# Moving the cache loads of a decode-attention kernel from GpSimd's DMA queue to SyncE's, and the last load of wo behind the last values

## The chip, the cores and the metric

The kernel runs on one core of a Trainium2 chip (eight cores, of which seven stay idle here). The metric is the device time of one execution in microseconds, as a median over runs. The profile is one further execution, recorded by the hardware profiler; its span runs from the first to the last instruction, so it is a little shorter than the execution itself.

## The reference

One decode step: one token of width D = 640 attends over a cache of 32768 positions in 32 heads of width 192, and then passes through a small dense block. Everything is bfloat16.

```python
x: (1, 1, 640)   k_cache, v_cache: (1, 32, 32768, 192)   wq: (640, 32*192)   wo: (32*192, 640)
w1: (640, 1536)  w2: (1536, 640)

q = (layernorm(x) @ wq).reshape(1, 1, 32, 192).transpose(0, 2, 1, 3)
scores = einsum("bhqd,bhkd->bhqk", q, k_cache) * 192 ** -0.5
o = einsum("bhqk,bhkd->bhqd", softmax(scores), v_cache)
h = x + o.transpose(0, 2, 1, 3).reshape(1, 1, 32 * 192) @ wo
h2 = h + relu(layernorm(h) @ w1) @ w2
```

The two caches are 805 MB of the 825 MB that the kernel reads. Each byte is used once, for one query.

## The kernel before

The work is staged head by head: `LAST` = 31 is the last of heads 0 to 31. Head h reads its keys in two loads, k(h,0) and k(h,1), of 6,144 KB each, into the buffers `kt[0]` and `kt[1]`, and its values in three: v(h,0) and v(h,1), of 3,072 KB each, both into the buffer `vb`, and v(h,2), of 6,144 KB, into `va`. There is one buffer of each, so a load waits until the work on what the buffer held is done. A head is computed in eight chunks c = 0 to 7, four on each key buffer. Of each chunk one part of the scores is formed on VectorE (`scores_dve`, L714 and L717: a product with the query, then a sum) and the other part on TensorE (`transposes` at L390, copied out of PSUM by ScalarE at L617, then `scores_pe`, recorded at L371). ScalarE forms the exponentials (L623 and L632), and TensorE multiplies them with the values (`values`, recorded at L371 with output `o_ps`); the end of that is the event PV(h,c). Chunks 0 and 1 use v(h,0), chunks 2 and 3 use v(h,1), chunks 4 to 7 use v(h,2). In head 0 the order of the values on TensorE is 0, 1, 4, 5, 2, 3, 6, 7 (`SUMS_0`).

All order is written out by hand. Each engine runs its own program, and `wait` names the event that it waits for. What matters here is the two programs without arithmetic:

- `relay_program`, on SyncE: first it issues seven loads (`first_loads`, L235): the five parts of wq, then k(0,0) and v(0,0). After that it waits for each load in turn and tells TensorE (L353) and VectorE (L332) that it has landed.
- `dma_program`, on GpSimd: after building an identity matrix it issues all other loads (L250), with `single_packet=True`, each behind the waits for its buffer.

The waits of the loads that the prediction follows are these. k(0,1) and v(0,2) wait until the queries are done (`att0`), since they overwrite wq. v(h,1) waits for PV(h,1). k(1,0) waits for PV(0,4) and for VectorE's chunk 3 of head 0 (`scs`). v(1,0) waits for PV(0,3). k(1,1) waits for PV(0,5) and VectorE's chunk 7.

wo comes in 16 loads of 480 KB into one buffer `wo_s`, one for every two heads, issued at the even heads. The last head has smaller pieces: keys k(31,0) to k(31,5), values v(31,0) and v(31,1), two halves of v(31,2) and four small pieces behind; then w1 and four parts of w2. Its program on TensorE (`pe_end`) ends with the projection through wo (`project`), the second norm, w1, and w2.

Of the kernel before, what the change touches and what calls it, by code (L numbers as in the profile page):

```python
# [7 lines left out]
A = mybir.AluOpType  # L8
# [72 lines left out]
def kernel(  # L81
# [12 lines left out]
    nc = tc.nc  # L94
    P = nc.NUM_PARTITIONS

    Bsz, Sq, D = A_x.shape
    _, H, Sk, Dh = A_k_cache.shape
# [6 lines left out]
    DT = D // P  # L105
    FT = Dff // P
    JK = 128
    JL = 64
    J = 32
    JPS = (20, 16)  # L110
    HE = Dh // 2
    NK = Sk // (P * JK)
# [3 lines left out]
    LAST = H - 1  # L116
# [26 lines left out]
    k_hd = A_k_cache.rearrange("b h s d -> (b h) s d")  # L143
    v_hd = A_v_cache.rearrange("b h s d -> (b h) s d")
    wq_view = A_wq.rearrange("(p c) n -> p (c n)", p=P)
    wo_view = A_wo.rearrange("(g p b) n -> g p b n", p=P, b=3)
# [4 lines left out]
    def sbuf(name, shape, dtype, align=32):  # L151
        return ctx.enter_context(nc.sbuf_tensor(name, shape, dtype, align_bytes=align))
# [5 lines left out]
    kt = [sbuf(f"kt{i}", [P, JK * Dh], bf16, 512) for i in range(NK)]  # L158
    va = sbuf("va", [P, JK * Dh], bf16, 512)
    vb = sbuf("vb", [P, JL * Dh], bf16, 512)  # L160
    wo_s = sbuf("wo_s", [P, 3, D], bf16, 512)
# [10 lines left out]
    wide = sbuf("wide", [P, HE + P + 2 * (P - HE)], bf16)  # L172
# [29 lines left out]
    wq_c = [kt[1][:, c * H * Dh:(c + 1) * H * Dh] for c in range(DT - 1)] + [va[:, 0:H * Dh]]  # L202
# [14 lines left out]
    def v_tile(h, ld):  # L217
        return v_at[ld] if h == LAST else (vb, vb, va)[ld][:]


    names = ["pool_pe", "act_pe", "dve_pe", "act_dve", "dve_act", "dve", "dve_row", "pe_dve", "pool_row", "pool_dve", "pool_act", "pe_act", "pe", "dve_sp", "act_row"]
    names += [f"dk{i}" for i in range(NK)] + ["dva", "dvb", "dk_first", "dv_first"] + ["dwo", "dx", "dout"] + [f"dwq{i}" for i in range(5)]
    names += [f"dke{i}" for i in range(4)] + ["dvh0", "dvh1"] + [f"dve{i}" for i in range(4)] + ["dw1"] + [f"dw2_{i}" for i in range(4)]
    sems = {n: nc.alloc_semaphore(n) for n in names}

# [1 line left out]
             "dve": ("pool_dve", "act_dve", "pe_dve", "dve")}  # L227


    def rows(src, h, k0, jl):  # L230
        return src[h, k0:k0 + P * jl, :].rearrange("(p j) d -> p (j d)", p=P)

    def first_loads(g):
        def load(dst, src, sem, *label):
            g.do(lambda: nc.sync.dma_start(out=dst, in_=src), sem, label, by=16)  # L235

        for c in range(DT):
            load(wq_c[c], wq_view[:, c * H * Dh:(c + 1) * H * Dh], f"dwq{c}", "wq", c)
        load(kt[0][:], rows(k_hd, 0, 0, JK), "dk_first", "k", 0, 0)
        load(vb[:], rows(v_hd, 0, 0, JK)[:, 0:JL * Dh], "dv_first", "v", 0, 0)  # L240

    def dma_program(g):
        e = nc.gpsimd
        g.do(lambda: e.memset(wide[:], 0.0), "pool_act", ("ident0",))
        g.wait("ident0")
        g.do(lambda: e.affine_select(out=wide[:], in_=wide[:], compare_op=A.not_equal, fill=1.0, base=HE,
                                     pattern=[[-1, HE + P + 2 * (P - HE)]], channel_multiplier=1), "pool_row", ("ident",))

        def load(dst, src, sem, *label):
            g.do(lambda: e.dma_start(out=dst, in_=src, single_packet=True), sem, label, by=16)  # L250

        def keys(h, ld):
            if h > 0:
                if ld == 0:
                    g.wait("PV", h - 1, 4 if h == 1 else 2)
                else:
                    g.wait("PV", h - 1, 5)
                g.wait("scs", h - 1, 4 * ld + 3)
            elif ld == 1:
                g.wait("att0")  # L260
            load(kt[ld][:], rows(k_hd, h, P * JK * ld, JK), f"dk{ld}", "k", h, ld)

        def vals(h, ld):

            if ld == 1:
                g.wait("PV", h, 1)
            elif h > 0:
                g.wait("PV", h - 1, 3 if ld == 0 else NC - 1)
            src = rows(v_hd, h, P * JK * (ld // 2), JK)
            if ld < 2:  # L270
                src = src[:, ld * JL * Dh:(ld + 1) * JL * Dh]
            load((vb, vb, va)[ld][:], src, "dva" if ld == 2 else "dvb", "v", h, ld)

        for h in range(LAST):
            if h > 0:
                keys(h, 0)
                vals(h, 0)
            keys(h, 1)
            for ld in ((2, 1) if h == 0 else (1, 2)):
                vals(h, ld)  # L280
            if h % 2 == 0:
                if h > 0:
                    g.wait("prj", h)
                load(wo_s[:], wo_view[h // 2], "dwo", "wo", h // 2)

        def end_keys(i, k0, jl, sem):
            load(k_at[i], rows(k_hd, LAST, k0, jl), sem, "k", LAST, i)

        def end_values(ld, c0, c1, sem, *label):
            load(v_at[ld][:, c0:c1], rows(v_hd, LAST, P * JL * ld, JL)[:, c0:c1], sem, *label)  # L290


        g.wait("PV", LAST - 1, 2)
        g.wait("scs", LAST - 1, 3)
        end_keys(0, 0, JL, "dk0")
        g.wait("PV", LAST - 1, 3)
        end_values(0, 0, JL * Dh, "dvb", "v", LAST, 0)
        end_keys(1, P * JL, JL, "dke0")
        g.wait("PV", LAST - 1, 5)
        g.wait("scs", LAST - 1, NC - 1)  # L300
        end_keys(2, 2 * P * JL, JL, "dk1")
        k0 = P * JL * (NL - 1)
        at = []
        for i, jl in enumerate(ENDJ):
            at.append((k0, jl))
            end_keys(NL - 1 + i, k0, jl, f"dke{1 + i}")
            k0 += P * jl
        g.wait("PV", LAST - 1, NC - 1)
        end_values(1, 0, JL * Dh, "dva", "v", LAST, 1)

        for i in range(2):
            end_values(2, i * J * Dh, (i + 1) * J * Dh, f"dvh{i}", "vh", i)
        i = 0
        for ld, (k0, jl) in enumerate(at):
            for c, (l, off, jc, *_) in enumerate(ends):
                if l == NL - 1 + ld:
                    g.wait("PV", LAST, 1)
                    load(v_tile(LAST, l)[:, off * Dh:(off + jc) * Dh],
                         rows(v_hd, LAST, k0, jl)[:, off * Dh:(off + jc) * Dh], f"dve{i}", "vc", LAST, c)
                    i += 1  # L320
        g.wait("PV", LAST, 3)
        load(w1_s, B_w1.rearrange("(c p) n -> p c n", p=P), "dw1", "w1")
        for i, (c0, c1) in enumerate(zip(W2_CUTS[:-1], W2_CUTS[1:])):
            load(w2_s[:, c0:c1], B_w2.rearrange("(c p) n -> p c n", p=P)[:, c0:c1], f"dw2_{i}", "w2", i)


    def relay_program(g):
        first_loads(g)

        def key(h, ld):  # L330
            relay(g, "k", h, ld)
            g.do(lambda: nc.sync.sem_inc(sems["pool_dve"], 1))  # L332
            book_relay(g, "k", h, ld, sem="pool_dve")

        for h in range(LAST):
            key(h, 0)
            relay(g, "v", h, 0)
            key(h, 1)
            for ld in ((2, 1) if h == 0 else (1, 2)):
                relay(g, "v", h, ld)  # L340
            relay(g, "W", h)
        key(LAST, 0)
        relay(g, "v", LAST, 0)
        key(LAST, 1)
        key(LAST, 2)
        relay(g, "v", LAST, 1)

    def relay(g, *label):
        if label[0] != "W":
            g.wait(*label)  # L350
        elif label[1] % 2 == 0:
            g.wait("wo", label[1] // 2)
        g.do(lambda: nc.sync.sem_inc(sems["pool_pe"], 1))  # L353
        book_relay(g, *label)

    def book_relay(g, *label, sem="pool_pe"):
        if g.planning:
            n = g.book["count"].get(sem, 0) + 1
            g.book["count"][sem] = n
            g.book["at"][("at" if sem == "pool_pe" else "atd",) + label] = (sem, n)  # L360
# [445 lines left out]

    book = {"count": {}, "at": {}}
    plan = Program(book, sems)
    for f in (relay_program, dma_program):
        f(plan)  # L810
    parts = {"pe": (pe_start, pe_head, pe_end), "act": (act_start, act_head, act_end), "dve": (dve_start, dve_head, dve_end)}
    logs, links = {}, {}
# [56 lines left out]
    with nc.Block(name="decode_blk", no_gpsimd_drain=True) as block:  # L869
        @block.sync  # L870
        def _(eng):
            relay_program(Program(book, sems, nc.sync))

        @block.gpsimd
        def _(eng):
            dma_program(Program(book, sems, nc.gpsimd))

        @block.scalar
        def _(eng):
            looped("act", nc.scalar)  # L880

        @block.vector
        def _(eng):
            looped("dve", nc.vector)

        @block.tensor
        def _(eng):
            looped("pe", nc.tensor)
# [34 lines left out]
```

## Time and profile before

| | |
|---|---|
| median of 4 runs | 1920.84 us (1919.93 to 1921.7) |
| the profiled execution | 1923.71 us, of which the span is 1921.8 us |
| busy share of the span | PE 81%, DVE 81%, PEld 57%, ACT 49%, POOL 5% |
| mean granted TensorE clock | 0.874 |
| read from HBM | 824.97 MB, 429 GB/s over the span |
| queue q0 (software_dynamic: GpSimd's) | 25984 packets, 807.68 MB, 97.4% of 16 DMA engines' span |
| queue q1 (hardware_dynamic: SyncE's) | 1008 packets, 17.30 MB, 2.1% |
| issue of one 6,144 KB load | 0.48 us on SyncE, 0.53 us on GpSimd |

PE is TensorE's matmuls, PEld its weight loads, DVE is VectorE, ACT ScalarE, POOL GpSimd, SP SyncE; a q behind a name (SPq) is the engine's sequencer, which handles waits and signals. Times in the rows are microseconds from the start of the span. "Idle before" is the time in which an engine stood still ahead of an instruction, with what released it. The chain is followed back from the last instruction: each step was released by the one before it.

### The profile page before, as it was taken

The page shows a single profiled execution, that of the slowest core. Times are in us where ns is not written, and L with a number is a line of the kernel's source. Part 1 is how long each engine was busy: PE and PEld are TensorE (multiplying, and loading weights), DVE is VectorE, ACT ScalarE, POOL GpSimd, SP SyncE. Part 2 cuts the span into 40 slices and gives each one's busy share as a digit, 9 for nine tenths or more (in the row PEclk, how much of TensorE's full clock was granted, in tenths as well). Part 3 has the DMA queues.
Part 4 walks back from the last instruction along what each step waited for, and adds up shares of the span by engine and source line. Part 5 has one row for each costly group of instructions (what it writes and reads, how often), then busy time and mean ns, then how long its engine had stood idle before and what let it go on. Part 6 is the DMA issues. An engine that isn't in the chain of part 4 may idle for free.

```text
span 1921.8 us, 36109 instructions
## 1 busy us (share of the span) xinstructions
PE 1560.9 (81%) x15899; PEld 1092.5 (57%) x15899; DVE 1561.3 (81%) x731; ACT 939.3 (49%) x2000; POOL 101.6 (5%) x194
## 2 busy tenths in 40 slices
PE   7687887888878888878878787788778787878888
PEld 7455555655555565555555555555555555555555
DVE  2888788987879878789787888878798787887896
ACT  1454454553545544545545445545355454454454
POOL 0000000000000000000000000000000000000011
PEclk9889988788988889888899888998888998888998
DMA  9999999999999999999999999999999999999998
GB/s 409 388 434 430 430 436 429 437 435 428 437 430 438 428 439 429 437 430 437 434 433 433 435 434 433 435 429 438 429 436 434 434 434 433 435 432 434 430 433 350
DMA packets 27026, 825.29 MB, mean 429 GB/s; under 512 B 3131, under 2 KB 3132, under 8 KB 5500
## 3 DMA queue, kind: packets, MB, share of 16 engines
q0 software_dynamic: 25984, 807.68, 97.4%
q1 hardware_dynamic: 1008, 17.30, 2.1%
q8 instruction: 15, 0.25, 0.0%
q14 instruction: 7, 0.06, 0.0%
q10 hardware_dynamic: 12, 0.00, 0.0%
HBM read 824.97 MB, written 0.00 MB: 429 GB/s over the span
## 4 chain that ended last, share of the span: by engine, by line
DVE 39%; DMA 36%; PE 16%; ACT 5%; issue 2%; another core or an unknown queue 1%; DVEq 0%; SPq 0%; POOL 0%
DMA kt<-in_A_k_cache_dram 36%; DVE sc L717 19%; DVE pr L714 18%; PE tp L390 8%; PE o_ps L371 7%; ACT kT L617 5%; PE sp L371 1%; DVE o_pair L729 1%; ACT pA L632 1%; DVE oT L739 0%; DVE rec L722 0%; DVE rec L723 0%; DVE odd L735 0%; DVE o_pair L741 0%
## 5 line engine op out<-in xcount | busy, mean ns | idle before, releaser
L714 DVE TENSOR_TENSOR pr<-kt,qb 128x2304 f32<-128x2304 bf16 (+2 forms) x257 | 756.7, 2944 | 318.9 <-SPq L332 290.8
L617 ACT COPY kT<-tp 128x1024 bf16<-128x1024 bf16 (+1 forms) x898 | 814.3, 1017 | 275.8 <-PE tp L390 275.8
L390 PE MATMUL tp<-ident_f,kt 128*128 128x128 f32 x3456 | 595.2, 333 | 240.8 <-SPq L353 165.6
L717 DVE TENSOR_REDUCE sc<-pr 128x12 f32<-128x2304 f32 (+2 forms) x257 | 756.1, 2942 | 8.9
L390 PEld LDWEIGHTS tp<-ident_f,kt 128*128 128x128 f32 x3456 | 488.4, 172 | 291.7 <-SPq L353 171.0
L371 PE MATMUL o_ps<-va,pB 128*2 128x384 bf16 x1152 | 219.2, 338 | 49.1 <-SPq L353 49.1
L371 PE MATMUL o_ps<-vb,pB 128*2 128x384 bf16 x1152 | 219.1, 337 | 34.7 <-ACT pA L632 20.4
L371 PEld LDWEIGHTS sp<-qm,kT 128*128 128x128 bf16 x6912 | 197.6, 98 | 83.7 <-issue 43.1
L371 PE MATMUL sp<-qm,kT 128*128 128x2 bf16 x6912 | 214.8, 164 | 25.4 <-ACT pB L623 24.0
L632 ACT ACTIVATE pA<-sc 128x12 bf16<-128x12 f32 (+2 forms) x257 | 58.1, 226 | 341.9 <-DVEq L65 341.9
L623 ACT ACTIVATE pB<-sp 128x20 bf16<-128x20 f32 (+2 forms) x258 | 52.4, 203 | 315.8 <-PE sp L371 315.8
L371 PEld LDWEIGHTS o_ps<-va,pB 128*2 128x2 bf16 x1152 | 93.7, 86 | 143.8 <-SPq L353 56.3
L371 PE MATMUL o_ps<-va,pA 128*2 128x384 bf16 x896 | 170.8, 332 | 0.0
L371 PEld LDWEIGHTS o_ps<-vb,pB 128*2 128x2 bf16 x1152 | 91.4, 86 | 139.0 <-ACT pA L632 27.4
L371 PE MATMUL o_ps<-vb,pA 128*2 128x384 bf16 x896 | 167.7, 327 | 0.0
L371 PEld LDWEIGHTS o_ps<-va,pA 128*2 128x2 bf16 x896 | 76.9, 86 | 74.7 <-issue 7.3
L371 PEld LDWEIGHTS o_ps<-vb,pA 128*2 128x2 bf16 x896 | 75.4, 84 | 70.9 <-issue 1.2
L250 POOL DMA_DIRECT2D kt<-in_A_k_cache_dram x67 | 35.6, 531 | 835.9 <-PE o_ps L371 804.6
L250 POOL DMA_DIRECT2D vb<-in_A_v_cache_dram x66 | 34.9, 529 | 811.5 <-PE o_ps L371 811.5
L623 ACT ACTIVATION_READ_ACCUMULATOR pB<-sp 128x1 f32 x258 | 55.1, 214 | 0.0
L632 ACT ACTIVATION_READ_ACCUMULATOR pA<-sc 128x1 f32 x257 | 53.0, 206 | 0.0
L371 PE MATMUL o_ps<-xn_ln,kt 128*96 128x1 bf16 (+1 forms) x316 | 22.3, 208 | 2.6 <-DMA kt<-in_A_wq_dram 2.6
(74 smaller groups left out, 260.0 us busy)
## 6 DMA issues: line engine op xcount, KB each, us to landing
kt<-in_A_k_cache_dram POOLq DMA_DIRECT2D x61, 6144.0 KB, 26.1
va<-in_A_v_cache_dram POOLq DMA_DIRECT2D x31, 6144.0 KB, 26.4
vb<-in_A_v_cache_dram POOLq DMA_DIRECT2D x62, 3072.0 KB, 13.2
kt<-in_A_k_cache_dram POOLq DMA_DIRECT2D x3, 3072.0 KB, 22.8
wo_s<-in_A_wo_dram POOLq DMA_DIRECT2D x16, 480.0 KB, 18.7
kt<-in_A_wq_dram SPq DMA_DIRECT2D x4, 1536.0 KB, 10.9
kt<-in_A_k_cache_dram SPq DMA_DIRECT2D x1, 6144.0 KB, 36.0
vb<-in_A_v_cache_dram SPq DMA_DIRECT2D x1, 3072.0 KB, 57.2
```

The source lines that it names most:

```text
L250: g.do(lambda: e.dma_start(out=dst, in_=src, single_packet=True), sem, label, by=16)
L371: return lambda: pe.matmul(o, lhsT=w, rhs=r, **kw)
L390: calls.append(lambda b=b, o=o: pe.transpose(out=dst[:, b, :], in_=src[:, o:o + 2 * P].bitcast(f32), identity=ident_f[:]))
L617: g.do(lambda: act.copy(out=kT[c % 2][:, b0:b0 + nb, :], in_=src[:, 0:nb, :].bitcast(bf16)), "act_pe", ("cp", h, c, k))
L623: g.do(lambda: act.activation(out=pB[c % NB][:, 0:jp], in_=sp[:, 0:jp], func=F.Exp, scale=SCALE, accum_out=dsums[:, 2 * c + 1:2 * c + 2]), ...
L632: g.do(lambda: act.activation(out=pA[c % NB][:, 0:jd], in_=sc[c % NC][:, 0:jd], func=F.Exp, scale=SCALE, accum_out=dsums[:, 2 * c:2 * c + ...
L714: g.chain(lambda: dve.tensor_tensor(out=pr[:, 0:j1 - j0, :], in0=src[:, (off + j0) * Dh:(off + j1) * Dh].rearrange("p (j d) -> p j d", d=D ...
L717: g.chain(lambda: dve.reduce_sum(out=sc[c % NC][:, j0:j1], in_=pr[:, 0:j1 - j0, :], axis=X), "dve")
L729: g.do(lambda: dve.tensor_scalar_mul(out=o_pair[:, :, 1, :], in0=o_ps[0:2, 0:2 * Dh].rearrange("q (i d) -> q i d", i=2), scalar1=rec[0:2, ...
```

## The change

All loads are issued by SyncE, without the flag, in one queue; the seven first ones stand at the head of the same program (`dma_program`), and their order and the order of all others is what it was. GpSimd takes over the relays (`pool_program`), behind its identity matrix. k(0,0) and v(0,0) lose their own semaphores and share those of the later loads of their buffers. The last load of wo, which was issued at head 30 ahead of k(31,0), is issued behind the last pieces of head 31's values and ahead of w1; the relay that head 30 sent for it no longer waits for it, and the projection at the very end waits for the load itself, as before.

```diff
-    def rows(src, h, k0, jl): ...
-    def first_loads(g):
+    def dma_program(g):
         def load(dst, src, sem, *label):
             g.do(lambda: nc.sync.dma_start(out=dst, in_=src), sem, label, by=16)
 
-        for c in range(DT):
-            load(wq_c[c], wq_view[:, c * H * Dh:(c + 1) * H * Dh], f"dwq{c}", "wq", c)
-        load(kt[0][:], rows(k_hd, 0, 0, JK), "dk_first", "k", 0, 0)
-        load(vb[:], rows(v_hd, 0, 0, JK)[:, 0:JL * Dh], "dv_first", "v", 0, 0)
-
-    def dma_program(g):
-        e = nc.gpsimd
-        (memset and affine_select of the identity)
-        def load(dst, src, sem, *label):
-            g.do(lambda: e.dma_start(out=dst, in_=src, single_packet=True), sem, label, by=16)
+        def rows(src, h, k0, jl): ...
...
+        for c in range(DT):
+            load(wq_c[c], wq_view[:, c * H * Dh:(c + 1) * H * Dh], f"dwq{c}", "wq", c)
         for h in range(LAST):
-            if h > 0:
-                keys(h, 0)
-                vals(h, 0)
+            keys(h, 0)
+            vals(h, 0)
             keys(h, 1)
             for ld in ((2, 1) if h == 0 else (1, 2)):
                 vals(h, ld)
-            if h % 2 == 0:
+            if h % 2 == 0 and h < LAST - 1:
                 if h > 0:
                     g.wait("prj", h)
                 load(wo_s[:], wo_view[h // 2], "dwo", "wo", h // 2)
...
+        g.wait("prj", LAST - 1)
+        load(wo_s[:], wo_view[H // 2 - 1], "dwo", "wo", H // 2 - 1)
         g.wait("PV", LAST, 3)
         load(w1_s, B_w1.rearrange("(c p) n -> p c n", p=P), "dw1", "w1")
...
-    def relay_program(g):
-        first_loads(g)
+    def pool_program(g):
+        (memset and affine_select of the identity)
         def key(h, ld):
             relay(g, "k", h, ld)
-            g.do(lambda: nc.sync.sem_inc(sems["pool_dve"], 1))
+            g.do(lambda: nc.gpsimd.sem_inc(sems["pool_dve"], 1))
...
-        elif label[1] % 2 == 0:
+        elif label[1] % 2 == 0 and label[1] < LAST - 1:
             g.wait("wo", label[1] // 2)
-        g.do(lambda: nc.sync.sem_inc(sems["pool_pe"], 1))
+        g.do(lambda: nc.gpsimd.sem_inc(sems["pool_pe"], 1))
...
         @block.sync
-            relay_program(Program(book, sems, nc.sync))
+            dma_program(Program(book, sems, nc.sync))
         @block.gpsimd
-            dma_program(Program(book, sems, nc.gpsimd))
+            pool_program(Program(book, sems, nc.gpsimd))
```

More of the change, by code (lines that the diff above doesn't have):

```diff
@@ L221 @@
     names = ["pool_pe", "act_pe", "dve_pe", "act_dve", "dve_act", "dve", "dve_row", "pe_dve", "pool_row", "pool_dve", "pool_act", "pe_act", "pe", "dve_sp", "act_row"]
-    names += [f"dk{i}" for i in range(NK)] + ["dva", "dvb", "dk_first", "dv_first"] + ["dwo", "dx", "dout"] + [f"dwq{i}" for i in range(5)]
+    names += [f"dk{i}" for i in range(NK)] + ["dva", "dvb"] + ["dwo", "dx", "dout"] + [f"dwq{i}" for i in range(5)]
     names += [f"dke{i}" for i in range(4)] + ["dvh0", "dvh1"] + [f"dve{i}" for i in range(4)] + ["dw1"] + [f"dw2_{i}" for i in range(4)]
@@ L227, with rows @@
              "dve": ("pool_dve", "act_dve", "pe_dve", "dve")}
-    def rows(src, h, k0, jl):
-        return src[h, k0:k0 + P * jl, :].rearrange("(p j) d -> p (j d)", p=P)
-    def first_loads(g):
+    def dma_program(g):
         def load(dst, src, sem, *label):
             g.do(lambda: nc.sync.dma_start(out=dst, in_=src), sem, label, by=16)
-        for c in range(DT):
-            load(wq_c[c], wq_view[:, c * H * Dh:(c + 1) * H * Dh], f"dwq{c}", "wq", c)
-        load(kt[0][:], rows(k_hd, 0, 0, JK), "dk_first", "k", 0, 0)
-        load(vb[:], rows(v_hd, 0, 0, JK)[:, 0:JL * Dh], "dv_first", "v", 0, 0)
-    def dma_program(g):
-        e = nc.gpsimd
[L244 to L247, printed above, removed]
-        def load(dst, src, sem, *label):
-            g.do(lambda: e.dma_start(out=dst, in_=src, single_packet=True), sem, label, by=16)
+        def rows(src, h, k0, jl):
+            return src[h, k0:k0 + P * jl, :].rearrange("(p j) d -> p (j d)", p=P)
         def keys(h, ld):
@@ L324, in dma_program @@
             load(w2_s[:, c0:c1], B_w2.rearrange("(c p) n -> p c n", p=P)[:, c0:c1], f"dw2_{i}", "w2", i)
-    def relay_program(g):
-        first_loads(g)
+    def pool_program(g):
+        e = nc.gpsimd
+        g.do(lambda: e.memset(wide[:], 0.0), "pool_act", ("ident0",))
+        g.wait("ident0")
+        g.do(lambda: e.affine_select(out=wide[:], in_=wide[:], compare_op=A.not_equal, fill=1.0, base=HE,
+                                     pattern=[[-1, HE + P + 2 * (P - HE)]], channel_multiplier=1), "pool_row", ("ident",))
         def key(h, ld):
             relay(g, "k", h, ld)
-            g.do(lambda: nc.sync.sem_inc(sems["pool_dve"], 1))
+            g.do(lambda: nc.gpsimd.sem_inc(sems["pool_dve"], 1))
             book_relay(g, "k", h, ld, sem="pool_dve")
@@ L808 @@
     plan = Program(book, sems)
-    for f in (relay_program, dma_program):
+    for f in (dma_program, pool_program):
         f(plan)
```

## The prediction

> **What bounds the kernel now.** I read the page first, then the same quantity in stretches of my own, then the chain in the first heads, then the end. The page's slices say that the DMA engines are busy throughout and move nearly the same in every slice but three:
>
> ```profile
> DMA  9999999999999999999999999999999999999998
> GB/s 409 388 434 430 430 436 429 437 435 428 437 430 438 428 439 429 437 430 437 434 433 433 435 434 433 435 429 438 429 436 434 434 434 433 435 432 434 430 433 350
> ```
>
> A slice is 48 us. The first holds the start, the last the end of the work; the second, at 388, is the odd one. The table by stretches, whose last three columns are TensorE's granted clock, the DMA engines' busy share and GB/s, takes it apart:
>
> ```profile
> 3.00:36.00 33.00, 27.32 (x341) 27.01 (x339) 1.33 (x8) 0.89 (x4) 1.22 (x2) 1.00 1.02 434
> 62.00:71.00 9.00, 9.00 (x67) 4.69 (x64) 8.57 (x4) 3.31 (x7) 0.00 (x0) 0.73 1.01 437
> 71.00:76.00 5.00, 4.37 (x77) 3.69 (x76) 4.96 (x2) 3.15 (x11) 1.06 (x2) 1.00 0.75 254
> 76.00:81.00 5.00, 4.43 (x56) 3.16 (x55) 4.82 (x3) 5.00 (x10) 0.00 (x0) 1.00 0.96 412
> 81.00:89.00 8.00, 8.00 (x100) 5.13 (x99) 7.07 (x3) 6.19 (x11) 0.53 (x1) 1.00 0.72 259
> 89.00:119.00 30.00, 26.48 (x251) 16.46 (x249) 15.74 (x9) 14.62 (x32) 1.05 (x2) 1.00 1.02 437
> ...
> 177.00:1828.00 1651.00, 1345.74 (x13609) 939.14 (x13608) 1372.12 (x622) 817.83 (x1743) 82.43 (x156) 0.87 1.00 433
> ```
>
> From 177 to 1828 us the transfers run at 433 GB/s, share 1.00: the queue never empties, and the time is bytes over rate. Only between 71 and 89 us does it run dry, twice. Lost: 5 x (1 - 254/433) = 2.1, 5 x (1 - 412/433) = 0.2, 8 x (1 - 259/433) = 3.2, together 5.5 us; the neighbouring rows count up to 437, and 30 x 4/433 = 0.3 of it comes back there: 5.2 us.
>
> Why it runs dry, the chain from 20 to 130 us tells (start, length, what):
>
> ```profile
> 3.40 36.04 DMA kt<-in_A_k_cache_dram
> ...
> 39.54 21.63 another core or an unknown queue
> ...
> 61.24 5.28 PE o_ps L371 x16
> ...
> 80.68 2.71 PE o_ps L371 x16
> 83.39 0.28 issue
> 83.67 19.00 DMA kt<-in_A_k_cache_dram
> ```
>
> and GpSimd's own timeline:
>
> ```profile
> 71.59 0.53 POOL L250 DMA_DIRECT2D vb<-in_A_v_cache_dram  x1 [37.14 <-PE o_ps L371]
> ...
> 83.67 0.53 POOL L250 DMA_DIRECT2D kt<-in_A_k_cache_dram  x1 [11.02 <-PE o_ps L371]
> ```
>
> The unknown step ending at 61.2 is v(0,0): issued at 3.92, its row of DMA issues gives 57.2 us to landing, 61.1. It waited so long because GpSimd issued k(0,1) and v(0,2), 12,288 KB, at 33.2 and 33.9 in the other queue, and both queues then shared the engines. PV(0,1) came late, so v(0,1) was issued only at 71.59 and k(1,0) at 83.67, both onto an empty queue.
>
> The end has another limit, the landing of k(31,1), behind which PE and ACT run as a chain to the last instruction:
>
> ```profile
> 1868.69 1.62 PE L390 MATMUL tp<-ident_f,kt 128*128 128x128 f32 x8 [1.81 <-SPq L353]
> ```
>
> PE stood still for 1.81 us before it.
>
> **The change part by part.** Sums are made against the profiled execution, 1923.71 us (span 1921.8 and 1.9 around it); the median of 1920.84 lies 2.87 below it, and I carry the difference over.
>
> *One queue for the first loads.* k(0,0) landed at 3.40 + 36.04 = 39.4 with some of the other queue's packets already between; now v(0,0), 3,072 KB, follows at once: 3.146 MB / 433 GB/s = 7.3 us, at most 46.7 instead of 61.1. PV(0,0) then starts when its exponentials exist (ACT L632 ends at 48.7), 12.3 us before 61.24, and v(0,1) is issued near 71.59 - 12.3 = 59.3. The bytes up to v(0,2) are the same, so that still lands at 33.91 + 40.1 = 74.0. v(0,1) thus queues 15 us early, and the first dry stretch, 2.1 us, goes.
>
> What is late next is k(1,0). It needs PV(0,4), which needs v(0,2): 74.0. The transposes ahead took 7.5 us in this head (73.1 to 80.6) and can start when k(0,1) has landed, 14.5 us before v(0,2), so they are done at 67. PV(0,4) takes 2.71 us (row 80.68) or, after idle time, 5.28 (row 61.24); with 0.28 of issue, k(1,0) is issued at 77.1 to 79.7. After 83.67 the DMA row in fine slices stands near zero until 84.9, so a start costs 1.2 us: first bytes at 78.3 to 80.9. v(0,1) and wo land on the last of the engines at 74.0 + 7.3 + 1.1 = 82.4; the fine slices fall from 9 about 2 to 3 us before the last landing, so the first engines run out at 79.4 to 80.4. Between nothing and 1.5 us is lost; since PE idles from 67 to 74, I lean to the slow row and take 0.5. Saved: 5.2 - 0.5 = 4.7 us. v(1,0) waits for PV(0,3), 12.3 us behind PV(0,4) before (95.7 against 83.4), now 92 at latest, while k(1,0) occupies the engines until about 95: no third dry stretch.
>
> *The queue of all later loads.* 188 loads move from POOL to SP with the same waits in the same order. Their issue (0.53 us there, 0.48 here) lies beside transfers. The rate of SP's queue is seen from 3 to 36 us, where it is alone: 434 GB/s against 433. Taken at nothing; bounds from the rivals. Cover is the queue that stands when a load is issued: v(1,1) at 119.26, while k(1,1), issued 96.51, lands 27.9 later, 124.4. Less 2 us of spread between engines and 1.2 of start, 2.0 us remain; heads 2 to 30 repeat the pattern at share 1.00.
>
> The Trainium skill speaks against a gain here: "DMA: Bandwidth & Descriptors", section "Issuing engines are not separate DMA queues", says that all issuers' transfers run on the same engines and that the choice saves only issue time. By that alone the sum would hold nothing but wo, 1919.7. Section "Queues, rings and completion order" of that page adds that an engine takes turns between its queues packet by packet, which is what v(0,0)'s 57.2 us look like; by it the two queues' order matters once, at the start.
>
> *Relays on POOL.* SP's relay shows 0.04 us between landing and PE (issue steps of the chain); POOL's wait until issue shows 0.28. In the heads the 2.0 us cover it; at the end it lies on the path. Between -0.1 and 0.3 us; I take 0.1 lost.
>
> *wo behind the values.* 480 KB / 433 GB/s = 1.1 us that no longer stands before k(31,0) to k(31,5) and the values. The chain from k(31,1) starts up to 1.1 us earlier; PE's 1.81 us of idle hold it, and the loads behind, which PE meets without waiting, come earlier too. DVE's own wait for k(31,0) is 1.66, and its query is ready 0.95 before its start, enough, since the chain's later waits for DVE have over 2 us to spare. wo itself lands about 6 us before its use at 1913.04 less 1.1. w1 and w2 hold their place in the bytes, so relative to them PE comes 1.1 us sooner: the last part of w2 lands about 1916.1 and is used from 1916.80 + 1.6 on, 2.3 us, of which 1.2 stay. The new wait for prj has nothing late behind it: that event, near 1828, is some 50 us old by then. Saved 1.1; bounds 0 and 1.3.
>
> Sum: 4.7 - 0.1 + 1.1 = 5.7 us. The profiled execution would take 1918.0 (span 1916.1), the median 1915.1.
>
> **The rivals.**
>
> *Slower: the loop of a head loses its cover.* Once per head v(h,1) meets a queue with 2.0 us to spare. If SyncE's wait and start, plus POOL's relay before it, take over 2.0 us more than now, the queue runs dry in each of 30 heads: at 2.5 us more, 30 x 0.5 - 5.7 = 9 us slower, 1930. It decides from 2.0 + 5.7/30 = 2.2 us. Against it: SP's first issue at 0.97 has the engines busy at 1.95, 1.0 us, less than POOL's 1.2. For it: no row shows SP issuing onto a queue at work behind a wait.
>
> *Slower: SP's queue is slower beside the computing,* or loses something between loads. 1% is 19 us: 1934; from 0.3% on it eats the gain. The 434 GB/s are of 33 us only, with DVE nearly idle.
>
> *No difference that can be measured.* The runs before spread by 1.8 us, so I call 0.2%, 3.8 us, what can be told from no change: 1917.0 to 1924.7. If the second dry stretch stays (3.2 us, k(1,0) issued some 3 us later than I think), the gain is 5.7 - 3.2 + 0.5 = 3.0: 1917.8. That the bytes are late anyway and only wo counts gives 1919.7.
>
> **How the numbers follow.** Forecast 0.64: its own range is 1914.2 (nothing lost at k(1,0), wo full, POOL's relay free: 6.6 saved) to 1917.0 (1.5 lost there, wo half, relay 0.3), with 1.2 below, 0.9 for the scatter of the runs and 0.3 should the 5.5 us of the table be right and not 5.2: 1913.0. No difference 0.16, loop 0.12, rate 0.08. Faster 0.64, same 0.16, slower 0.20. The range reaches from 1913.0 to 1921.0, over the cases of no difference, and leaves out the two slower ones, 0.20.
>
> **What would show it.** Right: between 60 and 120 us the GB/s stay at 433, v(0,0) lands by 46.7, v(0,1) is issued by SP near 59 and k(1,0) near 79, and PE's idle before the transposes of k(31,1) stays near 1.8 us or falls only where DVE or the relay is late. Wrong: rows under 430 GB/s in the middle stretch; if dips come once a head, at v(h,1), it is the loop; if the rate is lower without dips, the queue; if k(1,0) still meets an empty queue, the first step failed.

## The result

| | before | after |
|---|---|---|
| median | 1920.66 us (60 runs, 1918.22 to 1922.97) | 1917.43 us (40 runs, 1916.24 to 1919.31) |
| the profiled execution | 1923.71 us, span 1921.8 | 1917.47 us, span 1915.6 |
| ratio of the medians | | 0.9983, 95% interval 0.9979 to 0.9988 |

The change takes 3.2 us off, 2.3 to 4.0 by the interval. That is 0.17%: clear of noise with this many runs, but just under the 0.2% that the prediction took as the bound of what can be told. The median of 1917.43 also lies outside the forecast's own range (1913.0 to 1917.0, chance 0.64) and inside that of no difference (1917.0 to 1924.7, chance 0.16). The two profiled executions, however, lie 6.2 us apart, close to what was forecast (5.7). So there are two questions: whether the 6.2 us came from where the prediction said, and why the medians show half of it.

The page of after; the queue table now has SyncE's queue q1 for everything, and the second slice, which held 388 GB/s, is full at 429:

```profile
GB/s 409 429 433 432 430 439 426 439 434 430 435 433 433 435 434 429 436 431 437 433 432 435 432 433 435 432 430 436 430 437 436 430 437 431 434 433 434 431 433 367
...
q1 hardware_dynamic: 29616, 824.98, 99.8%
```

The table by stretches of after (last three columns: TensorE's granted clock, the DMA engines' busy share, GB/s):

```profile
3.00:36.00 33.00, 27.31 (x341) 27.00 (x339) 1.33 (x8) 0.89 (x4) 0.00 (x0) 1.00 1.02 434
...
62.00:71.00 9.00, 6.20 (x62) 4.43 (x60) 8.67 (x4) 9.00 (x16) 0.00 (x0) 0.88 1.01 438
71.00:76.00 5.00, 2.03 (x7) 0.84 (x8) 4.85 (x2) 1.24 (x2) 0.00 (x0) 0.50 0.90 382
76.00:81.00 5.00, 5.00 (x56) 3.17 (x54) 4.82 (x3) 1.38 (x6) 0.00 (x0) 0.83 1.17 476
81.00:89.00 8.00, 7.63 (x92) 4.50 (x91) 5.30 (x2) 3.31 (x13) 0.00 (x0) 1.00 0.95 400
89.00:119.00 30.00, 24.61 (x246) 16.79 (x244) 19.88 (x13) 14.14 (x28) 0.00 (x0) 0.94 0.99 425
...
177.00:1828.00 1651.00, 1345.32 (x13565) 938.82 (x13566) 1371.89 (x620) 820.81 (x1743) 0.00 (x0) 0.87 1.00 433
```

The queue of SyncE moves 433 GB/s through the whole middle, exactly as GpSimd's did. Between 71 and 119 us, where a packet counts in the row it falls into, the four rows together make 20.2 MB in 48 us, 422 GB/s: 1.3 us lost, where before lost 5.2.

The chain of after from 20 to 130 us, and SyncE's own timeline:

```profile
33.58 40.29 DMA va<-in_A_v_cache_dram
...
73.97 4.60 PE o_ps L362 x16
78.57 0.02 issue
78.58 19.62 DMA kt<-in_A_k_cache_dram
```

```profile
54.50 0.33 SPq L232 DMA_DIRECT2D vb<-in_A_v_cache_dram  x1
...
78.58 0.33 SPq L232 DMA_DIRECT2D kt<-in_A_k_cache_dram  x1
```

The step of 21.63 us for v(0,0) has left the chain. v(0,1) is issued at 54.50 instead of 71.59, k(1,0) at 78.58 instead of 83.67, behind v(0,2), which lands at 73.9 as it did before.

To see where each microsecond goes I use the first product on VectorE of head 2 and of head 30, which wait for k(2,0) and k(30,0). Before, then after:

```profile
160.92 2.56 DVE L714 TENSOR_TENSOR pr<-kt,qb 128x2304 f32<-128x2304 bf16 x1 [7.83 <-SPq L332]
...
1802.22 2.56 DVE L714 TENSOR_TENSOR pr<-kt,qb 128x2304 f32<-128x2304 bf16 x1 [7.75 <-SPq L332]
```

```profile
156.81 2.56 DVE L705 TENSOR_TENSOR pr<-kt,qb 128x2304 f32<-128x2304 bf16 x1 [8.16 <-POOLq L323]
...
1798.37 2.56 DVE L705 TENSOR_TENSOR pr<-kt,qb 128x2304 f32<-128x2304 bf16 x1 [7.74 <-POOLq L323]
```

They cut each span into three: start (to head 2), middle (head 2 to head 30) and end (from head 30). Before: 160.9, 1641.3 and 119.6. After: 156.8, 1641.6 and 117.2. So the profiled gain of 6.2 is 4.1 at the start, -0.3 in the middle, and 2.4 at the end.

### The profile page after: what moved, and what is told of

It is laid out like the page before. It is cut to its first block, busy times and chain, and to the rows that moved or that the text cites. A ratio compares the mean times of both kernels' runs of the same rounds, so it can differ in the third digit from the quotient of the medians.

```text
span 1915.6 us, 36109 instructions
## 1 busy us (share of the span) xinstructions
PE 1561.2 (82%) x15899; PEld 1093.0 (57%) x15899; DVE 1561.3 (82%) x731; ACT 939.4 (49%) x2000; POOL 1.0 (0%) x6
## 4 chain that ended last, share of the span: by engine, by line
DVE 39%; DMA 38%; PE 16%; ACT 5%; issue 1%; DVEq 0%; POOLq 0%; SPq 0%
DMA kt<-in_A_k_cache_dram 34%; DVE sc L708 18%; DVE pr L705 18%; PE o_ps L362 8%; PE tp L381 7%; ACT kT L608 5%; DMA va<-in_A_v_cache_dram 4%; PE sp L362 1%; DVE o_pair L720 1%; ACT pA L623 1%; DVE oT L730 0%; DMA kt<-in_A_wq_dram 0%; DVE rec L713 0%; DVE rec L714 0%; DVE odd L726 0%
## 5 line engine op out<-in xcount | busy, mean ns | idle before, releaser
L362 PE MATMUL o_ps<-va,pB 128*2 128x384 bf16 x1152 | 223.5, 342 | 57.4 <-POOLq L344 57.4
L362 PE MATMUL o_ps<-vb,pB 128*2 128x384 bf16 x1152 | 216.2, 334 | 22.4 <-ACT pA L623 21.8
L362 PEld LDWEIGHTS o_ps<-xn_ln,kt 128*96 128x96 bf16 (+1 forms) x316 | 22.1, 174 | 3.0 <-issue 2.9
L362 PEld LDWEIGHTS attT<-oT,wo_s 128*128 128x128 bf16 x465 | 19.5, 108 | 2.2 <-DVE oT L730 0.4
```

Source lines behind the costliest of these rows:

```text
L362: return lambda: pe.matmul(o, lhsT=w, rhs=r, **kw)
```

## The experiments

All were compared with the kernel before on the same chip, but not all on one chip: e1 to e4 ran on one, where the median of before was 1921.65, e5 to e8 on a second (1920.72), e9 to e12 on a third (1920.61). Across chips the ratios to before are the better comparison than the medians; a ratio is taken over all runs and need not be the quotient of the two medians. The same cuts, from the same rows of each profile:

| kernel | start | middle | end | profiled execution | median; ratio to before on the same chip (95% interval) |
|---|---|---|---|---|---|
| before | 160.9 | 1641.3 | 119.6 | 1923.71 | 1920.66 |
| before, second profile (e4) | 161.2 | 1641.3 | 117.6 | 1921.91 | |
| before, third (e11) | 159.6 | 1641.4 | 118.2 | 1921.07 | |
| before, fourth (e12) | 158.6 | 1641.6 | 117.3 | 1919.35 | |
| e6 before, no flag | 159.4 | 1641.3 | 116.8 | 1919.23 | 1920.36, 1.0 (0.9991 to 1.0008) |
| e1 before, wo moved | 159.0 | 1642.1 | 116.8 | 1919.73 | 1920.64, 0.9995 (0.9986 to 1.0004) |
| e3 nine first on SyncE | 164.7 | 1641.3 | 118.3 | 1926.09 | 1925.29, 1.0017 (1.0008 to 1.0026) |
| e8 eleven first on SyncE | 157.8 | 1642.7 | 117.2 | 1919.49 | 1919.8, 0.9995 (0.9986 to 1.0004) |
| e2 all SyncE, wo ahead | 156.5 | 1641.5 | 117.6 | 1917.52 | 1917.7, 0.9982 (0.9973 to 0.9991) |
| e5 after, two queues in head 0 | 157.5 | 1641.6 | 117.4 | 1918.38 | 1919.83, 0.9995 (0.9986 to 1.0003) |
| after | 156.8 | 1641.6 | 117.2 | 1917.47 | 1917.43, 0.9983 (0.9979 to 0.9988) |
| after, second profile (e9) | 156.5 | 1641.5 | 116.9 | 1916.71 | 1917.59, 0.9982 (0.9973 to 0.9991) |
| e7 after, k(1,0) early | 156.5 | 1641.5 | 116.3 | 1916.22 | 1916.71, 0.9978 (0.997 to 0.9987) |
| e10 the same again | 156.5 | 1641.5 | 117.8 | 1917.71 | 1916.31, 0.9978 (0.9969 to 0.9987) |

**e2: the change of queue alone.**

```diff
 (the kernel after)
-            if h % 2 == 0 and h < LAST - 1:
+            if h % 2 == 0:
-        g.wait("prj", LAST - 1)
-        load(wo_s[:], wo_view[H // 2 - 1], "dwo", "wo", H // 2 - 1)
-        elif label[1] % 2 == 0 and label[1] < LAST - 1:
+        elif label[1] % 2 == 0:
```

> The kernel after with the last load of wo back ahead of the last head's keys: the change of queue alone. Theory A: the queue's part is what the result is short of the sum, 1917.4 + 1.1 = 1918.5 us, 2.1 us under before (1.5 to 3); its profile shows the head-0 stretch as in the profile after (about 1.3 us lost between 71 and 119 us). Rival C (the queue's part is worth the 4 to 5 us that the profiles show, and moving wo costs 1 to 2 of it): 1916.0 or less, under the kernel after.

1917.7 us, ratio 0.9982: the queue alone (with the relays, which change engine with it) has, within the interval, all of the gain. Its start, 156.5, is that of after (156.8, and 156.5 in e9).

**e1: the move of wo alone.**

```diff
 (the kernel before)
-            if h % 2 == 0:
+            if h % 2 == 0 and h < LAST - 1:
+        g.wait("prj", LAST - 1)
+        load(wo_s[:], wo_view[H // 2 - 1], "dwo", "wo", H // 2 - 1)
         g.wait("PV", LAST, 3)
-        elif label[1] % 2 == 0:
+        elif label[1] % 2 == 0 and label[1] < LAST - 1:
```

> The kernel before with the last load of wo moved behind the last values, and nothing else. Theory A (the two parts add up, and each is worth what the profiles say): 1.1 us less than before, between 0.5 and 1.8, a ratio near 0.9994; in its profile TensorE no longer stands still, or under 0.8 us, ahead of the transposes of k(31,1), and the dry stretch between 71 and 89 us is as before. Rival B (the end is not worth anything in a run of ordinary length, since something else ends last there): 0 within 0.4 us.

0.9995, an interval that holds both 0 and 1.1 us: the timing does not decide. The profile says more. TensorE's wait ahead of the transposes of k(31,1), 1.81 before, is 0.65, 1.16 us less, which is the load's 1.1. But at the very end a new wait stands, for the parts of w2, which was hidden before (the second block gives the total, the number of waits and the longest):

```profile
1866.46 1.86 PE L392 MATMUL tp<-ident_f,kt 128*128 128x128 f32 x15 [0.65 <-SPq L355]
```

```profile
PE attT L373 <- DMA kt<-in_B_w_dram: 0.9, 3, 0.5
```

So 1.2 us earlier keys are answered by up to 0.9 us at w2, whose place in the bytes has not changed.

**e5: the shared start put back into after.**

```diff
 (the kernel after)
-            elif ld == 1:
-                g.wait("att0")
...
-            keys(h, 1)
-            for ld in ((2, 1) if h == 0 else (1, 2)):
+            if h > 0:
+                keys(h, 1)
+            for ld in ((1,) if h == 0 else (1, 2)):
...
 (in pool_program, ahead of the relays)
+        g.wait("att0")
+        (k(0,1) and v(0,2): e.dma_start(..., single_packet=True), semaphores of their own)
```

> The kernel after, but k(0,1) and v(0,2) alone are issued by GpSimd with the flag, ahead of its relays, as they were before: only the sharing of the engines by two queues in head 0 is put back. Theory A (the queue's gain is the order of head 0): 2 to 4 us over the kernel after, 1919.5 to 1921.5, close to the kernel before with only wo moved (1920.6); v(0,0) lands near 59 to 61 us, v(0,1) is issued at 69 to 72, k(1,0) at 81 to 84, and 3 to 5 us are lost between 71 and 119 us. Rival D (the gain comes from SyncE's queue over the rest of the time): within 0.7 us of the kernel after.

1919.83 us, 2.3 us over the two medians of after (1917.43 and 1917.59), as theory A had it. By the ratios, 0.9995 against 0.9983, it is 2.3 us as well; the two intervals meet only between 0.9986 and 0.9988. SyncE's timeline shows k(1,0) late again, though all of the other 30 heads are SyncE's:

```profile
68.84 0.33 SPq L232 DMA_DIRECT2D vb<-in_A_v_cache_dram  x1
...
80.92 0.33 SPq L232 DMA_DIRECT2D kt<-in_A_k_cache_dram  x1
```

Only two loads were put on the other queue, and by the medians that took back most of the gain. The profiled execution, 1918.38, was the fastest of this kernel's eleven, so its start of 157.5 shows less than its median.

**e3: nine first loads on SyncE.**

```diff
 (the kernel before, first_loads)
         load(vb[:], rows(v_hd, 0, 0, JK)[:, 0:JL * Dh], "dv_first", "v", 0, 0)
+        g.wait("att0")
+        load(kt[1][:], rows(k_hd, 0, P * JK, JK), "dk1_first", "k", 0, 1)
+        load(va[:], rows(v_hd, 0, P * JK, JK), "dva_first", "v", 0, 2)
...
 (dma_program no longer issues these two)
```

> The kernel before, but SyncE also issues k(0,1) and v(0,2), behind the same wait, so that the first nine loads stand in one queue; all later loads stay GpSimd's with the flag, the relays stay SyncE's. Theory A (all that the change of queue brings lies in the order of the first loads): the same time as the all-SyncE kernel with wo ahead, within 0.6 us, some 2 us under before; v(0,0) lands before 47 us, v(0,1) is issued near 55, k(1,0) near 79. Rival D (GpSimd's queue is slower or faster than SyncE's over the other 1800 us): it differs from that kernel by over 1 us.

A clear miss: 1925.29 us, slower than before. The edit cured the first sharing and made a second. v(0,1) and wo, now issued at 54.84 by GpSimd, shared the engines with v(0,2), still at work on SyncE's queue. The chain of this kernel:

```profile
33.26 48.08 DMA va<-in_A_v_cache_dram
81.38 0.04 issue
81.43 5.24 PE o_ps L372 x16
86.67 0.28 issue
86.95 18.91 DMA kt<-in_A_k_cache_dram
```

v(0,2) landed at 81.3 instead of 73.9, 7.4 us late, about the 7.3 us that v(0,1) takes by itself. PV(0,4) waits for v(0,2), k(1,0) for PV(0,4), so k(1,0) was issued at 86.95, and the queue was dry for longer than before:

```profile
76.00:81.00 5.00, 0.00 (x0) 0.00 (x0) 4.82 (x3) 0.00 (x0) 0.00 (x0) 0.50 0.83 353
81.00:89.00 8.00, 7.57 (x61) 4.10 (x62) 5.35 (x2) 1.28 (x5) 0.53 (x1) 0.66 0.35 108
```

With e8 below, which moves v(0,1) and that wo to SyncE's queue as well, this is the strongest evidence for the mechanism: what costs is that a later issue on a second queue takes its share from a load whose landing is waited for.

**e8: all of head 0 on SyncE, the rest GpSimd's.**

```diff
 (e3, relay_program)
             relay(g, "v", h, 0)
+            if h == 0:
+                g.wait("PV", 0, 1)
+                (v(0,1) and the first wo: nc.sync.dma_start, semaphores of their own)
             key(h, 1)
...
 (dma_program no longer issues these two)
```

> The kernel before, but all of head 0's loads and the first wo, eleven, are SyncE's, in one queue; GpSimd issues from k(1,0) on, with the flag; relays stay SyncE's, the last wo stays ahead of the last head's keys. So the start is that of the all-SyncE kernel with wo ahead (1917.7), and the queue of the other heads is GpSimd's. Theory A (after head 0 the two queues are worth the same): 1917.7 within 0.8 us, k(1,0) issued near 79. Rival D (GpSimd's queue costs or saves in the other 30 heads or at the end): over 1 us away from it.

1919.8 us: 5.5 us under e3 by the medians, 4.2 by the ratios, so the second sharing is cured too, but 2.1 over e2 (2.5 by the ratios), outside theory A's 0.8. k(1,0) is issued at 79.56 (e2: 79.29) but takes 20.12 us to land instead of 18.23 (18.20 to 19.62 in the two profiles of after), and the start ends 1.3 us later than e2's; the rest stands in its middle, 1642.7 against 1641.3 to 1641.6 in most profiles. Those of e8 and e1 (1642.1), both GpSimd's, are the only long ones. The intervals of e8 and e2 overlap, so a part of the gain that lies in the queue itself, up to 2 us, is not excluded; what would make it is open.

**e6: the flag alone.**

```diff
 (the kernel before)
-            g.do(lambda: e.dma_start(out=dst, in_=src, single_packet=True), sem, label, by=16)
+            g.do(lambda: e.dma_start(out=dst, in_=src), sem, label, by=16)
```

> The kernel before without the flag of one packet per DMA and engine; queues and order as they were. Theory A (two queues take turns descriptor by descriptor whether the flag is set or not; v(0,0)'s 57 us fit turns of one of its rows for one of the other's): no difference from before, within 1 us, v(0,0) landing at 59 to 61. Rival G (with the flag a whole load is one turn, so that without it the sharing or the rate changes): v(0,0) lands over 4 us earlier or later, and the time moves by over 2 us.

Ratio 1.0, middle 1641.3, v(0,0) landed by 59.5, as in one profile of before with the flag (e12, 59.3): the flag does nothing here that these runs can tell, neither to the rate nor to how two queues take turns.

**e4, e11, e12: before, profiled three times more.**

> The kernel before, unchanged, profiled once more. Its first profile was of an execution of 1923.71 us, above all 60 timed runs (1918.22 to 1922.97). Theory E (chance of that execution): this one lies near 1920.7, and loses less than 5.2 us between 71 and 119 us. Rival F (recording makes this kernel longer by some 3 us whenever it is recorded): near 1923.7 again, with the same two dry stretches.

> The kernel before, a third profile. Theory E (executions of this kernel differ at the start and at the end: k(1,0) is issued anywhere from 81.7 to 83.7, set by when the last of the 16 engines finishes v(0,0), and the end behind k(31,0) takes 65 to 68 us): a value in these ranges, and a time that follows the two. Rival F (recording lengthens it): near 1923.7, with 83.7 and 67.8.

> The kernel before, a fourth profile, as the third: theory E expects k(1,0) issued between 81.7 and 83.7 and a time between 1919 and 1923 that moves with it; rival F expects 1923.7 each time.

GpSimd's issue of k(1,0) in the three, in this order:

```profile
83.61 0.53 POOL L250 DMA_DIRECT2D kt<-in_A_k_cache_dram  x1 [11.02 <-PE o_ps L371]
```

```profile
82.65 0.53 POOL L250 DMA_DIRECT2D kt<-in_A_k_cache_dram  x1 [11.02 <-PE o_ps L371]
```

```profile
80.68 0.53 POOL L250 DMA_DIRECT2D kt<-in_A_k_cache_dram  x1 [11.02 <-PE o_ps L371]
```

The idle of 11.02 us ahead of it is the same each time: the sequence behind v(0,1) slides as a whole. Two things move it, and the chains of e11 (first row) and e12 (the other two) separate them:

```profile
61.23 4.29 PE o_ps L371 x16
```

```profile
3.40 34.15 DMA kt<-in_A_k_cache_dram
...
59.35 4.20 PE o_ps L371 x16
```

In e11, k(0,0) took 36.04 us and v(0,0) landed at 61.2, as in the first profile and in e4; TensorE's first group of values took 4.29 us instead of 5.28, and that is the one microsecond. In e12 that group took 4.20, and k(0,0) landed 1.9 us earlier, and v(0,0) with it. The packets of the traces show why. Each of the 16 DMA engines writes 4 bytes behind its last row of a load, and the load has landed with the last of these 16 writes. In the first profile, e4 and e11 all rows of k(0,0) were in by 37.1 to 37.2 us, but one engine's write came only at 38.9 to 39.0, behind a 48 KiB row of the other queue (1.815 us); in e12, e1, e5 and e6 it came at 37.0 to 37.2. From there v(0,0)'s last write follows after 21.77 us in all seven profiles, which fits eight turns of one 24 KiB row of v(0,0) (0.912 us) for one 48 KiB row of the other queue: 8 x (0.912 + 1.815) = 21.8.

Between 71 and 119 us the four lost 5.2, 5.0, 4.4 and 2.4 us against 433 GB/s. The four executions of before took 1923.71, 1921.91, 1921.07 and 1919.35, with starts of 160.9, 161.2, 159.6 and 158.6 and ends of 119.6 to 117.3. Theory E holds for the times, but e12's 80.68 fell below its 81.7, and e4's start was as slow as the first one's (two dry stretches, 5.0 us lost). Recording does not by itself make 1923.7: three of the four lie within the 60 timed runs. Executions differ, and the first one profiled was slow both at its start and at its end.

**e9: after, profiled and timed again.**

> The kernel after, unchanged, on the chip of the next kernel, so that the two can be set side by side. Theory A: 3 to 4 us under before, ratio 0.998 to 0.9985; k(1,0) issued near 78.6, 1 to 1.5 us lost between 71 and 119 us. Rival: a profile of another execution of this kernel differs from the first by over 1 us at the landing of k(1,0), as those of the kernel before do among each other.

1917.59 us, k(1,0) at 79.25. Its start is 156.5, 0.3 from the first; that of before varied by 2.6. The times scatter less too: 40 runs of after lie within 3.1 us, 60 of before within 4.8. That this comes from the sharing is not shown, since e2, also with one queue, has a run of 1921.33 among its eleven.

**e7 and e10: k(1,0) issued earlier.**

```diff
 (the kernel after)
-                    g.wait("PV", h - 1, 4 if h == 1 else 2)
+                    g.wait("PV", h - 1, 1 if h == 1 else 2)
```

> The kernel after, but k(1,0) waits for PV(0,1) in place of PV(0,4): TensorE's last transposes from its buffer stand ahead of PV(0,1), and VectorE's chunk 3 is waited for as before. Theory A (what is still lost between 71 and 119 us is the late issue of k(1,0), 78.58): it is issued near 62, nothing is lost there (433 GB/s from 71 to 119), and 1.2 us are gained on the kernel after: 1916.2 (1915.7 to 1916.9). Rival H (the next load, v(1,0), or the end then becomes late): the stretch fills but the time gains less than 0.4 us, 1917.0 or more.

> The kernel after with k(1,0) issued behind PV(0,1), once more, beside the kernel after on one chip. Theory A: 0.5 to 1.2 us under the kernel after. Rival H (what head 0 gives is taken back at the next load): within 0.3 us of it.

k(1,0) goes out at 62.16, and the dip is gone (71 to 130 us: 432 GB/s, in after 429). The medians, 1916.71 and 1916.31, are the lowest of all kernels, 0.7 to 1.3 us under after's; the intervals overlap (0.9969 to 0.9987 here, 0.9973 to 0.9991 for e9). The cut at head 2 stands at 156.5, as in e9, so by the profile the filled dip is given back there, as rival H has it. A gain of about 1 us is likely and not shown.

## Why the prediction was right or wrong

**The start: right, step by step; its size was that of one execution (see below).** v(0,0) was to land by 46.7; issued at 4.04, it took 40.9 us: 44.9. v(0,2) at 74.0: 73.9. v(0,1) was to be issued near 59.3; it was 54.50, since k(0,0) landed 1.9 us earlier than in the first profile of before and TensorE's first group of values took 2.70 us instead of 5.28, at a granted clock of 1.00 (46.9 to 54.5 us) instead of 0.72 (61.0 to 71.6); nothing hung on that. PV(0,4) took 4.60 us, between the 2.71 and 5.28 of the two rows; k(1,0) was to go out at 77.1 to 79.7, and did at 78.58. Lost after it: 1.3 us, inside the 0 to 1.5, at 0.5 taken. The saving of 4.7 was 4.1 at head 2 in the profiled pair.

**The queue of the later loads: right.** 1641.6 against 1641.3 us over 28 heads, and 433 against 433 GB/s. Both slower rivals fall: neither the cover of a head nor the rate was touched.

**The relay:** the chain's steps show 0.02 + 0.03 + 0.04 us from landing to TensorE where GpSimd relays. The 0.04 that the prediction read for SyncE was the last of these steps alone: with SyncE, e3's chain shows 0.02 + 0.02 + 0.04. The difference is 0.01 us; 0.1 had been set aside.

**wo: the mechanism was right, what became of it was not.** Counted from the cut at head 30, the transposes of k(31,1) begin after 66.5 us in all eight profiles with wo ahead, and after 65.3 in four of the six with wo moved (e1, e5, e7, e9): the keys come 1.2 us earlier. TensorE's idle ahead of them falls with it, to 0.65 to 0.67 us; the prediction's sign, that it stays near 1.8, contradicted its own term. In the other two, after's first profile and e10, the transposes begin after 66.2. There TensorE itself was late, and I had checked the waits one by one only. In after's first profile it waits 2.82 us for v(30,2) and then takes 2.86 us for a part of its work that takes 1.78 in e9; in e10 the two groups of values just ahead took 2.26 and 2.39 us, in e9 1.46 each. So it was not ready for k(31,1) any sooner. Two rows of after's first profile, then e9's:

```profile
1841.85 2.86 PE L362 MATMUL o_ps<-va,pB 128*2 128x384 bf16 x10 [2.82 <-POOLq L344]
```

```profile
1864.55 1.84 PE L381 MATMUL tp<-ident_f,kt 128*128 128x128 f32 x15
```

```profile
1863.36 1.85 PE L381 MATMUL tp<-ident_f,kt 128*128 128x128 f32 x15 [0.67 <-POOLq L344]
```

And w2, to which I gave 1.2 us to spare, is waited for in just the four profiles with the earlier transposes: `attT` waits 0.9 us in e1, 1.2 in e5, 1.3 in e7 and 0.3 in e9. The ends average 117.8 us over the eight profiles with wo ahead and 117.1 over the six with wo moved: 0.8 us, a size that the ends' own scatter (116.3 to 119.6) nearly covers.

**The step that failed is "the median lies 2.87 below it, and I carry the difference over".** It took the terms of one profile as those of every run. The 5.2 us lost at the start and the end of 119.6 belong to an execution that was slower than each of the 60 timed ones. Over four profiles of before the loss between 71 and 119 us was 5.2, 5.0, 4.4 and 2.4 us, 4.3 in the mean, and over two of after 1.3 and 1.2: a gain of 3.0, not 4.7. By the cuts, the means are 160.1 against 156.7 at the start, 1641.4 against 1641.5 in the middle, and 118.2 against 117.0 at the end: 3.4 and 1.1 us gained, 0.2 lost, together 4.4 before rounding. So the term of the start was mis-sized by 1.3 to 1.7 us. The medians say 3.2 (2.3 to 4.0). Of the 1.2 us between the two, 0.85 is that before's four profiled executions average 1921.51, above the median of the 60 runs, and 0.34 that after's two average 1917.09, below the median of the 40. How much of the end's 1.1 a usual run keeps is open: e2, without the move of wo, has the ratio of after. The sign and the place were right; the claim that the gain would clear 0.2% was not. That 1917.43 lies in the whole range, up to 1921.0, is owed to its part for no measurable difference. (The upper bound of the forecast's own range comes to 1916.9 by its terms, not 1917.0.)

The rule of the Trainium skill that I set against the change ("DMA: Bandwidth & Descriptors", section "Issuing engines are not separate DMA queues") said that the issuer saves only issue time; the middle bears it out to 0.2 us in 1641. But two issuers at once do more than that: e3 against e8, and e5 against after, show 4 and 2 us by the ratios from nothing but which of two queues two loads stand in. The turns by packets that the section "Queues, rings and completion order" of that page describes are the better guide; in this case's traces a turn fits one row of a load, and leaving out the flag (e6) changed nothing that the runs can tell.

## What to carry to other kernels

Two queues that feed the same DMA engines do not move more, they only decide who waits: a load that is issued later on another queue takes its share from the one that is waited for now. Keep loads with a chain behind them in one queue, in the order in which they are needed, and before splitting loads over issuers look at the landing of the earlier one, not at the rate. And take a term of a few microseconds from several profiles, or set its size by the spread of the runs, when the profiled execution stands outside them.

## What was not expected

- The last of 16 DMA engines decides when a load has landed, and where two queues shared the engines, one engine's closing write behind a row of the other queue made k(0,0) 1.9 us late in three profiles of seven. That and TensorE's pace moved head 0: the same program issued k(1,0) at 83.67, 83.61, 82.65 and 80.68 us.
- The flag of one packet per DMA and engine changed nothing that the runs can tell (ratio 1.0, 0.9991 to 1.0008), also where two queues shared.
- The end's length went with TensorE's granted clock: from 1890 to 1905 us it was 0.79 in before's first profile and 0.90 in its second, and the ends were 119.6 and 117.6 us long. Over the stretch from 64 to 116 us behind the cut at head 30 the eight profiles with wo ahead had clocks of 0.82, 0.84, 0.84, 0.85, 0.85, 0.89, 0.90 and 0.91, and ends of 119.6, 118.2, 118.3, 117.6, 117.6, 117.2, 117.3 and 116.8 us. That the clock is the cause is argued, not shown.
